# Loading the first weight matrix by three groups in halves, and solving the order table again

## The chip, the cores and the metric

The kernel runs on one core of a Trainium2 chip. The metric is the time of one execution in microseconds (us) on the device; the median of several executions stands for a kernel. The profile comes from one such execution, and its span is some 1.8 us shorter than the time. All runs told of here are runs of one core, in the state that the records call fast.

## The reference, cut to what matters

```python
q_s = exp(q - max(q, -1));  q_s /= sum(q_s, -1)      # softmax over d
k_s = exp(k - max(k, 2));   k_s /= sum(k_s, 2)       # softmax over the sequence
kv  = einsum('bhsd,bhse->bhde', k_s, v)
x   = einsum('bhsd,bhde->bhse', q_s, kv)             # -> [4608 tokens, 512]
h   = x @ w_in                                       # [512, 2048], called W1 below
g   = where(h > 0, h, exp(min(h, 0)) - 1)            # ELU
out = g @ w_out                                      # [2048, 512], called W2 below
```

q, k and v are [8, 8, 576, 64] in fp32. The two products with W1 and W2 are nearly all of the work: 576 matmuls of 128x512 each.

## The kernel before

The tokens go through in 9 blocks of 512. In each block, W1's 2048 columns are 8 groups of 256. A group is 8 matmuls into PSUM, an exp on ACT, and one or two operations on DVE that make GT, the input of the product with W2. Block 0 is special: W1 is still being loaded. Its first two groups are split in two halves over the inner dimension, so that PE can start with the half of x (XT) that is ready first, and with the half of W1 that lands first.

```python
# program(): q, k, v of the first two units on SP's queue, then W1 on POOL's
for g0, g1, half in ((0, 2, 0), (0, 2, 1), (2, 5, None), (5, 8, None)):
    self.load_w1(g0, g1, half, -30, [gate, self.ident] if half == 0 else ())
# ... (load_w1 makes two transfers of each entry: eight in all)
key = 0
turns = [3, 1, 2, 0, 3, 1, 0, 2]                 # PSUM buffers of the groups
for half in range(2):
    for g in range(2):
        self.hg_mm(0, g, turns[g], key, half)    # the two split groups
for g in range(8):
    self.hg(0, g, turns[g], key, "da"[g % 2], g > 1)
    # ...
```

The program only lists operations. In which order each engine runs them is in a table, one list of operation numbers for each engine, that an offline solver made from assumed durations:

```python
ORDER = {
    "pe": ("30 28 32 45 43 47 50 67 54 68 69 70 77 81 85 92 114 102 89 128 136 ..."),
    "dve": ("4 0 5 2 6 7 25 26 27 37 38 39 40 41 42 36 46 49 51 52 53 56 72 73 ..."),
    # ... act, gp, sp
}
```

`fill()` walks through that order with the same assumed durations and, where PE would idle early on, puts in spare 128x128 matmuls of the identity (no result is used) to keep PE's clock up. `spare_after` names what they wait for:

```python
S.spare_after = [self.ident]
# fill(), for each PE operation o until the first large matmuls:
idle = o.start - free - 150
count = int(idle / 80)
if count > 1 and all(d.end < free for d in self.spare_after):
    p = Op("pe", count * 57, self.spare(count), 0)
```

Of the kernel before, what the change touches and what calls it, by code (L numbers as in the profile page):

```python
# [21 lines left out]
ISSUE = {"sp": 550, "act": 550, "gp": 740}  # L22
ORDER = {
    "pe": (
        "30 28 32 45 43 47 50 67 54 68 69 70 77 81 85 92 114 102 89 128 136 127 135 129 137 106 130 "
        "138 108 149 151 125 148 156 133 131 155 150 139 157 152 145 172 174 158 171 173 232 238 237 "
        "236 243 191 242 244 250 249 248 200 255 256 202 262 254 261 211 267 260 266 268 320 312 308 "
        "349 219 332 316 324 390 337 279 328 281 333 411 341 290 345 398 298 350 403 394 416 399 437 "
        "407 424 412 429 361 420 363 425 478 433 372 499 380 438 486 491 482 504 487 512 495 449 525 "
        "500 451 517 508 513 460 571 521 468 563 526 567 576 572 597 584 580 589 537 602 585 593 610 "  # L30
        "539 635 598 548 606 643 555 611 648 639 644 656 652 621 669 623 657 661 665 674 682 687 631 "
        "678 633 670 695 708 691 700 683 704 713 696 734 721 739 717 709 726 730 747 722 760 743 735 "
        "752 765 748 756 773 761 778 769 774 786 782 787 791 792 796 800 804 "),
    "act": (
        "3 22 33 23 24 29 31 34 35 44 48 55 71 74 75 78 82 83 86 93 94 96 103 115 90 91 118 97 116 "
        "107 126 119 132 134 159 162 178 153 146 179 165 229 168 230 175 204 187 233 239 240 190 272 "
        "245 251 252 201 214 257 203 210 263 212 264 283 217 216 321 313 269 213 309 220 354 317 278 "
        "325 292 293 280 391 338 329 289 334 282 295 296 342 291 346 365 351 299 360 395 375 417 442 "
        "404 400 377 374 408 413 362 421 364 378 426 371 479 373 430 434 381 453 439 483 463 492 530 "
        "505 488 448 465 496 466 450 501 459 518 452 509 514 461 462 522 469 564 541 527 568 577 573 "  # L40
        "536 551 615 581 550 603 590 538 586 594 625 540 553 547 636 554 549 599 607 612 556 640 620 "
        "645 649 622 653 624 662 666 658 630 632 675 688 679 671 692 684 701 714 705 697 634 718 740 "
        "710 727 731 723 744 736 753 749 757 766 762 770 779 775 783 788 793 797 801 805 807 "),
    "dve": (
        "4 0 5 2 6 7 25 26 27 37 38 39 40 41 42 36 49 46 51 52 53 56 72 73 76 79 80 84 87 88 95 99 "
        "104 105 100 101 121 117 109 122 110 111 123 140 141 142 154 147 181 182 183 231 176 177 205 "
        "234 235 192 206 193 241 194 207 195 196 246 197 247 253 273 274 275 258 259 265 270 284 271 "
        "285 310 311 286 221 355 222 223 224 225 226 318 319 326 327 330 356 331 335 336 357 343 344 "
        "347 348 352 366 353 300 396 301 302 367 397 401 368 402 303 304 409 410 305 414 415 443 422 "
        "444 423 427 428 445 435 436 454 382 440 455 383 384 441 385 386 484 456 485 387 489 490 497 "  # L50
        "498 531 502 503 510 511 515 516 523 532 524 533 528 529 470 569 570 542 574 471 472 575 473 "
        "543 474 475 544 582 583 587 595 588 616 596 617 618 600 601 608 609 626 613 614 557 558 641 "
        "642 559 560 561 646 562 627 647 654 628 655 659 667 668 660 680 681 672 673 693 694 685 686 "
        "706 707 698 699 719 720 711 712 732 733 724 725 745 737 738 746 750 751 758 759 763 764 771 "
        "772 776 777 784 785 "),
    "gp": (
        "1 14 15 16 17 18 19 20 21 57 59 58 60 63 61 62 66 98 64 65 112 113 124 120 144 143 180 185 "
        "188 "),
    "sp": (
        "8 9 10 11 12 13 184 186 161 164 163 170 167 189 199 198 208 166 169 160 209 215 276 277 315 "  # L60
        "227 218 314 287 228 288 294 358 393 297 359 339 322 323 340 306 307 405 369 376 392 406 370 "
        "379 418 432 419 447 480 481 431 446 388 389 464 507 458 506 493 457 494 520 476 566 477 535 "
        "534 467 565 519 545 546 604 552 578 591 579 619 592 650 637 605 638 629 651 690 676 663 664 "
        "677 703 715 702 689 742 716 755 754 741 728 729 767 768 781 780 789 795 790 794 803 799 802 "
        "798 806 "),
}


# [171 lines left out]
class Gen:  # L240
# [85 lines left out]
    def load_w1(self, g0, g1, half, key, after=()):  # L326
        w = self.w_in.rearrange("(h kc d) f -> h d kc f", h=2, d=D)
        sl = slice(g0 * 256, g1 * 256)
        ks = slice(0, 4) if half is None else slice(2 * half, 2 * half + 2)
        xs = (0, 1) if half is None else (half,)  # L330
        for h in range(2):
            self.S.add("gp", ISSUE["gp"], lambda e, h=h: e.dma_start(  # L332
                self.W1[h:128:2, ks, sl], w[h, :, ks, sl]), key,
                W=[f"W1_{g}{x}{h}" for x in xs for g in range(g0, g1)],
                dma=f"w1{g0}{xs[0]}{h}", nbytes=(len(xs) * (g1 - g0) << 17) * (1.15 if g0 == 2 else 1), after=after,
                follow=self.gpq)
            self.gpq = self.S.ops[-1]

# [281 lines left out]
    def program(self):  # L620
# [7 lines left out]
            if (n, t) == (0, "k"):  # L628
                gate = S.ops[-1]
        loaded = S.ops[-1]  # L630
        for g0, g1, half in ((0, 2, 0), (0, 2, 1), (2, 5, None), (5, 8, None)):
            self.load_w1(g0, g1, half, -30, [gate, self.ident] if half == 0 else ())
            S.ops[-2].behind = loaded
        AB, C, D_ = 3, 2, 1
# [100 lines left out]
        def piece(blocks):  # L735
            if steps:
                for n, go in steps.pop(0):
                    go()
# [6 lines left out]
        key = 0  # L745
        turns = [3, 1, 2, 0, 3, 1, 0, 2]
        for half in range(2):
            for g in range(2):
                self.hg_mm(0, g, turns[g], key, half)
        for g in range(8):  # L750
            self.hg(0, g, turns[g], key, "da"[g % 2], g > 1)
            if g == 4:
                self.side(AB, key, self.ao_mm(0, 1, AB), self.ao_mm(1, 1, AB, 64))
                self.xt(0, 1, AB, key)
                self.xt(1, 1, AB, key, at=64)
            key += 1
            if g >= 5:
                piece(0)
# [79 lines left out]
```

## Time and profile before

| what | where read | value |
|---|---|---|
| time, median of 3 runs | times | 301.82 us |
| PE busy | engine shares | 285.5 of 300.2 us |
| full clock granted | clock record | 12.80 us |
| first matmul with W1 | PE's timeline | 14.78 us |
| wait for W1 | PE's waits | 1.28 us, to 20.96 us |
| group 3 of block 0 starts | PE's timeline | 22.92 us |
| group 6 of block 1 starts | PE's timeline | 66.68 us |
| last large matmul starts | PE's timeline | 296.26 us |

The first matmul with W1 and the last three rows are the ruler of this study. At each of these places the same number of matmuls with W1 has been done in every kernel below, and from group 3 of block 0 to group 6 of block 1 all 14 profiled kernels have the same 88 matmuls with W1, 78 with W2 and 176 small ones to do. So a difference between two of these places is lost or gained in between.

The way in is the PE engine: it is busy 95% of the span, so look only for what it waits for. How the transfers are cut is in the list of DMA issues of the kernel before (operands, queue, count, size of one, median us from issue to landing):

```profile
W<-in_moe_w_in_dram POOLq DMA_DIRECT2D x4, 768.0 KB, 10.3
...
W<-in_moe_w_in_dram POOLq DMA_DIRECT2D x4, 256.0 KB, 4.9
```

The four small ones are the halves of groups 0 and 1; the four large ones are groups 2 to 4 and 5 to 7. The wait of 1.28 us is for the second of the large ones.

### The profile page before, as it was taken

What the parts mean: (1) busy time and instruction counts of PE and PEld (TensorE: products, weight loads), DVE (VectorE), ACT (ScalarE), POOL (GpSimd) and SP (SyncE); (2) the same over time, 40 slices, a digit from 0 to 9 for tenths busy, and PEclk for the clock granted to TensorE, in tenths of its full rate; (3) what the DMA queues carried; (4) which work ended last, traced back from release to release, by engine and by line L of the source; (5) the groups of instructions that cost most, each with busy time, mean ns of one, the idle gap of its engine ahead of it and who ended that gap; (6) DMA issues with size and microseconds to landing.
All of it is one profiled execution on the core that took longest, in us unless ns stands there. A gap on an engine that the chain in (4) does not pass through costs nothing.

```text
span 300.2 us, 4404 instructions
## 1 busy us (share of the span) xinstructions
PE 285.5 (95%) x1846; PEld 234.1 (78%) x1846; DVE 188.8 (63%) x244; ACT 181.5 (60%) x211; POOL 22.1 (7%) x33
## 2 busy tenths in 40 slices
PE   0789999999999999999999999999999999999995
PEld 0658877878888888888888888888888888888883
DVE  2957954898496768766767783878355436565500
ACT  5847948989868676673966677835441623434211
POOL 0950155100000000000000000000000000000000
PEclk9999999999999999999999999999999999999999
DMA  7999996999367593569931958203221201031224
GB/s 263 387 382 391 389 359 234 309 284 265 105 212 240 126 311 70 188 143 239 295 67 41 261 149 227 59 2 70 59 58 29 61 11 35 0 90 38 49 52 105
DMA packets 35283, 49.96 MB, mean 166 GB/s; under 512 B 16320, under 2 KB 16320, under 8 KB 35264
## 3 DMA queue, kind: packets, MB, share of 16 engines
q1 hardware_dynamic: 29680, 34.09, 41.0%
q0 software_dynamic: 5504, 15.47, 15.9%
q8 instruction: 14, 0.23, 0.3%
q10 hardware_dynamic: 80, 0.13, 0.1%
q14 instruction: 5, 0.04, 0.0%
HBM read 36.70 MB, written 9.44 MB: 154 GB/s over the span
## 4 chain that ended last, share of the span: by engine, by line
PE 88%; DMA 5%; DVE 4%; POOL 1%; ACT 1%; SPq 0%; issue 0%
PE PS L588 43%; PE PS L543 40%; DMA W<-in_moe_w_in_dram 3%; PE PS L487 3%; DMA KR<-in_k_dram 2%; PE PS L456 1%; DVE GT L578 1%; POOL W L332 1%; DVE ESB L576 1%; DVE QS L380 0%; DVE ZQ L372 0%; DVE GT L572 0%; DVE MBLK L469 0%; ACT ESB L559 0%; PE PS L403 0%; SPq L315 0%
## 5 line engine op out<-in xcount | busy, mean ns | idle before, releaser
L543 PE MATMUL PS<-XT,W 128*128 128x512 f32 x576 | 140.8, 391 | 1.9 <-DMA W<-in_moe_w_in_dram 1.3
L588 PE MATMUL PS<-W,GT 128*128 128x512 f32 x576 | 141.2, 391 | 0.0
L543 PEld LDWEIGHTS PS<-XT,W 128*128 128x128 f32 x576 | 106.9, 188 | 25.1 <-DMA W<-in_moe_w_in_dram 1.7
L588 PEld LDWEIGHTS PS<-W,GT 128*128 128x128 f32 x576 | 107.1, 188 | 21.9 <-DVE GT L572 0.3
L559 ACT ACTIVATE ESB<-PS 128x1024 f32<-128x1024 f32 x72 | 73.6, 1027 | 68.9 <-PE PS L543 67.1
L576 DVE TENSOR_SCALAR ESB<-ESB 128x1024 f32<-128x1024 f32 x64 | 44.1, 691 | 73.3 <-ACT ESB L559 72.8
L578 DVE TENSOR_TENSOR GT<-ESB,PS 128x1024 fp32r<-128x1024 f32 x64 | 77.8, 1218 | 1.8
L605 ACT ACTIVATE OSB<-PS 128x512 f32<-128x512 f32 x32 | 18.6, 596 | 23.8 <-PE PS L588 23.8
L509 ACT ACTIVATE XT<-PS 128x512 fp32r<-128x512 f32 (+6 forms) x32 | 19.4, 609 | 16.5 <-PE PS L487 14.7
L372 DVE TENSOR_REDUCE ZQ<-QR 128x18 f32<-128x1152 f32 x16 | 21.5, 1346 | 5.0 <-ACT QR L352 4.9
L380 DVE TENSOR_TENSOR QS<-QR,RZQ 128x1152 f16<-128x1152 f32 x16 | 21.7, 1356 | 0.3
L352 ACT ACTIVATE QR<-QR 128x1152 f32<-128x1152 f32 x16 | 18.6, 1161 | 3.1 <-DMA QR<-in_q_dram 3.1
L356 ACT ACTIVATE KR<-KR 128x1152 bf16<-128x1152 f32 x16 | 18.5, 1160 | 0.5 <-DMA KR<-in_k_dram 0.5
L487 PE MATMUL PS<-qsT,MBLK 128*128 128x320 f32 (+5 forms) x64 | 14.2, 307 | 0.1
L431 ACT ACTIVATE qsT<-QT 128x1152 fp32r<-128x1152 f16 x12 | 14.0, 1166 | 0.3 <-DMA QT<-QS 0.3
L365 ACT ACTIVATE VB<-VR 128x1152 bf16<-128x1152 f32 (+1 forms) x12 | 13.5, 1125 | 0.8 <-DMA VR<-in_v_dram 0.8
L487 PEld LDWEIGHTS PS<-qsT,MBLK 128*128 128x128 f32 x64 | 11.4, 190 | 3.1 <-DVE MBLK L469 1.1
L572 DVE SCALAR_TENSOR_TENSOR GT<-PS,ESB 128x1024 fp32r<-128x1024 f32 x8 | 9.8, 1222 | 3.6 <-ACT ESB L570 3.6
L403 PE MATMUL PS<-ID,QS 128*128 128x128 f16 x36 | 3.2, 244 | 9.1 <-DVE QS L380 9.1
L403 PEld LDWEIGHTS PS<-ID,QS 128*128 128x128 f16 x36 | 2.5, 112 | 9.6 <-DVE QS L380 9.1
L469 DVE TENSOR_TENSOR MBLK<-PS,RZK 64x128 fp32r<-64x128 f32 x32 | 9.1, 283 | 0.8
L570 ACT ACTIVATE ESB<-ESB 128x1024 f32<-128x1024 f32 x8 | 8.4, 1056 | 0.2
(28 smaller groups left out, 58.8 us busy)
## 6 DMA issues: line engine op xcount, KB each, us to landing
out_dram<-OSB SPq DMA_DIRECT2D x63, 128.0 KB, 2.4
QR<-in_q_dram SPq DMA_DIRECT2D x12, 576.0 KB, 4.9
KR<-in_k_dram SPq DMA_DIRECT2D x12, 576.0 KB, 5.8
VR<-in_v_dram SPq DMA_DIRECT2D x12, 576.0 KB, 5.6
W<-in_moe_w_out_dram POOLq DMA_DIRECT2D x4, 1024.0 KB, 19.3
W<-in_moe_w_in_dram POOLq DMA_DIRECT2D x4, 768.0 KB, 10.3
QR<-in_q_dram POOLq DMA_DIRECT2D x4, 576.0 KB, 11.1
KR<-in_k_dram POOLq DMA_DIRECT2D x4, 576.0 KB, 6.0
```

What stands on the lines that cost most here:

```text
L352: S.add("act", t_act(1152, False), lambda e: e.activation(flat(q), flat(q), AF.Exp), key - 3, X=[f"qR{i}"], follow=self.table)
L356: S.add("act", t_act(1152, False), lambda e: e.activation(ek[:, :, :, :].rearrange("p h c d -> p (h c d)"), flat(k), AF.Exp), key - 2, X=[ ...
L372: S.add("dve", t_dve(1152), lambda e: e.tensor_reduce(self.ZQ[i][:, :, :].rearrange("p h c -> p (h c)"), q[:, :, :, :].rearrange("p h c d ...
L380: S.add("dve", t_dve(1152), lambda e: e.tensor_tensor(qso, q[:, :, :, :], rz, ALU.mult), key - 3, R=[f"qR{i}", f"RZQ{i}"], W=[f"QS{self.al ...
L487: last = e.matmul(P[:, y:y + n_], M[:, f, :], T[:, c0:c1, f * 64:f * 64 + 64], start=True, stop=True)
L509: S.add("act", t_act((h1 - h0) * n_, True), lambda e, dst=dst, src=src: e.activation(dst, src, AF.Copy), key, W=W, X=X)
L543: last = e.matmul(P[:, t * 512:(t + 1) * 512], self.W1[:, kc, tt * 128:(tt + 1) * 128], self.XT[:, kc, rc:rc + BLK], start=(kc == 0), stop ...
L559: S.add("act", t_act(1024, True), lambda e: e.activation(esb[:, :], P[:, :], AF.Exp), key, W=[f"E{i}"], X=banks)
L576: S.add("dve", t_dve(1024, 2), lambda e: e.tensor_scalar(esb[:, :], esb[:, :], 1.0, -1.0, ALU.min, ALU.add), key, X=[f"E{i}"])
L578: S.add("dve", t_dve(1024), lambda e: e.tensor_tensor(gt, esb[:, :], P[:, :], ALU.max), key, R=[f"E{i}"], W=gw, X=banks)
L588: last = e.matmul(dst, GT[:, jj, ts * 128:(ts + 1) * 128], self.W2[:, jj, :], start=(jj == 0), stop=(jj == 15))
L605: S.add("act", t_act(512, True), lambda e: e.activation(osb[:, :], src, AF.Copy), key, W=[f"O{i}0", f"O{i}1"], X=[f"b{bk}"])
```

## The change

PE has done two groups when it must wait for groups 2 to 4. With three groups in the small transfers it has three groups of work before it needs the next transfer, and that next one is smaller. The order table is solved again, with assumed durations in which the loads of W1 may come later.

```diff
-        for g0, g1, half in ((0, 2, 0), (0, 2, 1), (2, 5, None), (5, 8, None)):
+        for g0, g1, half in ((0, 3, 0), (0, 3, 1), (3, 5, None), (5, 8, None)):
...
-   nbytes=(len(xs) * (g1 - g0) << 17) * (1.15 if g0 == 2 else 1)
+   nbytes=(len(xs) * (g1 - g0) << 17) * (1.25 if g0 == 3 else 1)
...
-            for g in range(2):
+            for g in range(3):
                 self.hg_mm(0, g, turns[g], key, half)
...
-            self.hg(0, g, turns[g], key, "da"[g % 2], g > 1)
+            self.hg(0, g, turns[g], key, "da"[g % 2], g > 2)
...
-    "dve": "4 0 5 2 6 7 25 26 27 37 38 39 40 ...
+    "dve": "2 4 5 0 6 7 25 26 37 27 38 39 40 ...   (all five lists are new)
```

`nbytes` only feeds the assumed durations. On DVE, 26 is the reciprocal of the first q's sums, 27 the first scaled q (QS), 37 the second q's sum (ZQ).

> **What bounds the kernel now.** I read the page first (engine shares and the clock row), then the chain of work that ended last, then the waits of PE, then PE's and DVE's timelines of the first 21 us and of 52 to 69 us, and the landing marks of the W1 transfers.
>
> ```profile
> PE 285.5 (95%) x1846; PEld 234.1 (78%) x1846; DVE 188.8 (63%) x244; ACT 181.5 (60%) x211; POOL 22.1 (7%) x33
> ...
> PE PS L588 43%; PE PS L543 40%; DMA W<-in_moe_w_in_dram 3%; PE PS L487 3%; DMA KR<-in_k_dram 2%; PE PS L456 1%; DVE GT L578 1%; POOL W L332 1%; DVE ESB L576 1%; DVE QS L380 0%; DVE ZQ L372 0%; DVE GT L572 0%; DVE MBLK L469 0%; ACT ESB L559 0%; PE PS L403 0%; SPq L315 0%
> ```
>
> PE is the bound, and the chain has little else in it. That a busy PE has little slack is only shown by spacing: the chain's last PE piece is
>
> ```profile
> 280.33 16.33 PE PS L588 x72
> ```
>
> 72 matmuls in 16.33 us, 0.227 us each. The 1152 large matmuls at that pace are 261 us, and nothing in this change alters their number. So the time can only move by what PE idles. PE's waits:
>
> ```profile
> PE PS L403 <- DVE QS L380: 9.1, 1, 9.1
> ...
> PE PS L543 <- DMA W<-in_moe_w_in_dram: 1.3, 1, 1.3
> PE PS L543 <- DVE XT L512: 0.4, 1, 0.4
> PE PS L543 <- DVE GT L578: 0.2, 1, 0.2
> ```
>
> The reader is to see four waits only: 9.1 us before the first real matmul, 0.4 at 14.8 us, 1.3 for a W1 transfer, 0.2 at 66.7 us. Where they lie:
>
> ```profile
> 14.78 1.16 PE L543 MATMUL PS<-XT,W 128*128 128x512 f32 x4 [0.42 <-DVE XT L512]
> 16.05 0.74 PE L487 MATMUL PS<-qsT,MBLK 128*128 128x512 f32 x2
> 16.63 3.05 PE L543 MATMUL PS<-XT,W 128*128 128x512 f32 x12
> 20.96 11.20 PE L543 MATMUL PS<-XT,W 128*128 128x512 f32 x48 [1.28 <-DMA W<-in_moe_w_in_dram]
> ```
>
> At 19.5 us PE has done the two split groups (16 matmuls) and waits for the load of groups 2-4, of which the second transfer lands at 20.92. From 20.96 to 66.5 us there is no wait over 0.15 us, and none from 66.7 us to the end.
>
> **What the Trainium skill says.** "DMA: Bandwidth & Descriptors", Issuing engines are not separate DMA queues: all transfers run on the same 16 DMA engines and interleave, whoever issues them. The trace agrees: from 1 to 25 us the DMAs move about 390 GB/s, and W1's eight transfers land one behind the other (13.01, 13.67, 14.37, 15.02, 17.70, 20.92, 22.88, 24.83 us), although all are issued by 13.2 us. So other cuts of the same bytes change which bytes come first, not when the last come. "Perfetto Trace Analysis", DMA Optimizations: splitting transfers may let some work start sooner, if the engines are idle; here they are not. "TensorE: Matmul & The Clock Gate", Part 1: PE runs at half clock until it was busy for a window of some 3.4 us, and that window runs freely. The trace agrees: the first transpose is at 9.12 us, the clock is granted at 12.80 us, and the spacing of transposes falls from 107 to 56 ns there.
>
> **The change part by part.** Of the 1.3 us: W1's first two groups become three, loaded by halves. Bytes before group 5 are the same (5 groups), so groups 3-4 land where groups 2-4 landed, near 20.9 us (the last of 16 engines is 1.3 us behind the others there, because one 16 KB instruction fetch of 1.03 us sits on it at 18.4 us; I take it that this stays). But PE now has 24 matmuls to do before it needs them, not 16: 8 x 0.227 = 1.8 us more. In the old order group 2 then took 20.96 to 22.92, so group 3 began at 22.92. If the front did not slip, group 3 could begin at 19.5 + 1.8 = 21.3 us: 1.6 us sooner, and no wait for W1.
>
> The halves are half as big again. First halves: 0.79 MB behind the six q/k/v loads (last landed 12.33 us) at about 0.39 MB/us land near 14.3 us, second halves near 16.3 us. They are needed at 14.8 and 17.6 us or later: hidden. Groups 5-7 land at 24.83 us as before; they were needed at 26.56 us and now near 25.2 us: still hidden, by 0.4 us.
>
> The front slips, because the new order table changes DVE's first work. Before:
>
> ```profile
> 6.02 1.35 DVE L372 TENSOR_REDUCE ZQ<-QR 128x18 f32<-128x1152 f32 x1 [4.41 <-ACT QR L352]
> 7.41 0.27 DVE L376 RECIPROCAL RZQ<-ZQ 128x18 f32<-128x18 f32 x1
> 7.71 1.36 DVE L380 TENSOR_TENSOR QS<-QR,RZQ 128x1152 f16<-128x1152 f32 x1
> 8.98 1.35 DVE L372 TENSOR_REDUCE ZQ<-QR 128x18 f32<-128x1152 f32 x1
> ```
>
> Now the second reduce goes ahead of the first QS: QS ends 1.35 us later, at 10.45, and the first transposes begin near 10.5 us, not 9.1. I walk on with the durations of the old trace. The copies of qsT end near 12.4, ACT's exp of the second k 13.45, the second kv product starts near 14.2 (was 13.88). On DVE the copy of qsT now comes before that of XT: XT is ready at 15.2, so the first group starts at about 15.3 (was 14.78). The m step of the second pair ends near 16.2 (was 16.0), and its product starts near 16.3 (was 16.05). From there PE is dense: slip 0.27 us. Group 3 begins at about 21.6 us: **1.3 us gained**.
>
> One loss may come on top. The spare matmuls that keep PE's clock up are placed by the table's planned times: before, 10 of them stood behind the first transposes; now 12 stand ahead of them and wait for nothing but the identity (ready at 1.5 us), so they run at once and warm nothing. With real work from 10.5 us the full clock comes at 13.9 us at the earliest (10.5 + 3.4), perhaps a window later. Each large matmul at half clock costs 0.2 us more; the four of the first group and the product are exposed, at most 0.9 us. If the grant falls anywhere in 13.9 to 17.3 us alike, my estimate is 0.25 us on average. Before, such a loss was swallowed by the 1.28 us wait; now it is not.
>
> Then the stretch from 46 to 67 us. PE comes sooner; do the others follow? The transfers come in a fixed stream: W2's third part lands at 39.01, needed near 39.5; the fourth moves behind k3, to about 43.1, needed at 44.4. Hidden. But block 1 is reordered. Before, group 1 ended first, then 0, 2 and 3 ran without a break. Now out products stand between groups 2 and 3, and need group 0's GT: group 0 ends near 52.1, exp 1.03, min 0.69, max 1.22 with hops give 55.25, and PE is there at about 54.85: 0.4 us of wait. Group 3 needs group 1's buffer, free after another 1.22 us at 56.5: 0.35 us of wait. DVE was all but full here (13.65 of 15 us busy from 52 to 67 us), so it gives little back:
>
> ```profile
> 65.08 0.30 DVE L469 TENSOR_TENSOR MBLK<-PS,RZK 64x128 fp32r<-64x128 f32 x1
> 65.40 1.22 DVE L578 TENSOR_TENSOR GT<-ESB,PS 128x1024 fp32r<-128x1024 f32 x1
> 66.86 1.23 DVE L572 SCALAR_TENSOR_TENSOR GT<-PS,ESB 128x1024 fp32r<-128x1024 f32 x1 [0.23 <-ACT ESB L570]
> ```
>
> The old waits here (0.1 and 0.33 us) fall away. New waits 0.85, old 0.4: about 0.45 us given back. Behind 67 us PE was dense and stays so; same work, same tail.
>
> Sum: -1.3 (W1 wait) + 0.25 (clock) + 0.45 (block 1) = -0.6 us. 301.82 - 0.6 = **301.2 us**.
>
> **The rivals.** (1) The whole 1.6 us is kept: block 1's order was solved with shifted loads in mind, and the walk's waits of 0.3 to 0.4 us are near its error. Against it are DVE's full 52 to 67 us. It would make 300.3. (2) The wait is turned into others: a cold start and DVE in block 1 eat it all. For it speaks that the old order left PE only 0.33 us idle in block 1; against it that each loss is bounded. It would make 301.8 to 302.2. (3) The fetch falls elsewhere and W1 groups 3-4 land 1.5 us sooner: no gain, PE isn't ready before 21.6. (4) A later reordering opens waits behind 67 us; the old trace had none there, each would add some 0.3 us.
>
> **Range and chances.** The floor is PE: even without any of the waits behind 14.8 us (1.3 + 0.4 + 0.2 = 1.9 us) it is 299.9. So faster by over 2% (295.8) is out of reach. Slower by over 2% needs 6 us of new waits; only a bad order over many blocks could do that. Range 300.3 to 302.0, from rivals 1 and 2.
>
> **What would show it right or wrong.** PE's waits no longer list W1 with 1.3 us (or under 0.3). The first transposes start near 10.5 us, the first large matmul near 15.3, group 3 near 21.6. The clock row's grant is at 13.9 us or later. From 52 to 67 us PE idles 0.6 to 1.2 us, on GT of DVE. Behind 67 us nothing. It is wrong if PE still waits for W1, if the front slips by over 1 us, or if waits stand behind 70 us.

## The result, and the profile after

The changed kernel took **301.64 us** (median of 6 runs, 301.10 to 302.35), the kernel before 301.83 in the same rounds (301.77 to 302.95). The ratio is 0.9989, with a 95% interval of 0.9970 to 1.0008: the same. A ratio here is the mean time of one kernel's fast runs over that of the other's of the same rounds, so it is not quite the ratio of the medians.

The first lines of the page of the changed kernel, engine shares and the chain that ended last:

```profile
PE 286.4 (95%) x1849; PEld 235.0 (78%) x1849; DVE 189.3 (63%) x244; ACT 182.1 (61%) x211; POOL 21.7 (7%) x33
...
PE PS L588 44%; PE PS L543 43%; PE PS L487 3%; DMA W<-in_moe_w_in_dram 2%; DMA KR<-in_k_dram 2%; PE PS L456 2%; POOL W L332 1%; ACT ESB L559 1%; DVE GT L572 0%; ACT ESB L570 0%; PE PS L403 0%; SPq L315 0%; ACT OSB L605 0%
```

By engine, PE's share of the chain went from 88 to 91% and DVE's from 4 to 0. PE's waits in the changed kernel (line waited at, releaser, us in total, times, longest):

```profile
PE PS L403 <- DVE QS L380: 6.6, 1, 6.6
PE PS L653 <- POOL ID L293: 1.9, 1, 1.9
PE PS L543 <- DMA W<-in_moe_w_in_dram: 0.6, 1, 0.6
PE PS L588 <- DVE GT L578: 0.4, 1, 0.4
PE PS L543 <- DVE XT L512: 0.3, 1, 0.3
```

The reader is to see that the wait for W1 has not gone: 1.3 became 0.6. The wait of the first line is shorter than before only because 12 spares now run ahead of it, at 1.9 us, as soon as the identity is there. And a wait of 0.4 for GT is new. Where these lie is in PE's timeline of the changed kernel (start, length, operation; in brackets the idle time before it and what ended that):

```profile
9.94 1.14 PE L403 MATMUL PS<-ID,QS 128*128 128x128 f16 x9 [6.60 <-DVE QS L380]
...
15.09 1.20 PE L543 MATMUL PS<-XT,W 128*128 128x512 f32 x4 [0.29 <-DVE XT L512]
16.12 0.63 PE L487 MATMUL PS<-qsT,MBLK 128*128 128x512 f32 x2
16.59 1.07 PE L543 MATMUL PS<-XT,W 128*128 128x512 f32 x4
18.23 2.09 PE L543 MATMUL PS<-XT,W 128*128 128x512 f32 x8 [0.57 <-DMA W<-in_moe_w_in_dram]
...
55.71 1.19 PE L588 MATMUL PS<-W,GT 128*128 128x512 f32 x4 [0.39 <-DVE GT L578]
56.99 1.21 PE L543 MATMUL PS<-XT,W 128*128 128x512 f32 x4
```

The wait is no longer for groups behind the split ones. It is at 18.2 us, inside the split groups, for their **second half**. The landing marks say why. A transfer is spread over 16 DMA engines. Fifteen of them had the second half in by 16.4 us; the last landed at 17.99. One engine had been a microsecond behind most of the others since 7.5 us: two packets, at 5.6 and 6.2 us, took 529 and 622 ns, and two more took 538 and 688 ns in this transfer. (The trace gives no engine's number with a packet; that these packets are all that one engine's is inferred from their times.)

The Trainium skill, "DMA: Bandwidth & Descriptors", Why a DMA increments its semaphore by 16 and not by 1, says that the engines finish independently and that only the full count means that all data has landed. The trace agrees, and puts a size to it: the slowest engine of one transfer came more than 1.5 us behind the other fifteen.

Against the ruler:

| place | before | changed | difference |
|---|---|---|---|
| full clock granted | 12.80 | 13.67 | |
| first matmul with W1 | 14.78 | 15.09 | +0.31 |
| group 3 of block 0 | 22.92 | 21.99 | -0.93 |
| group 6 of block 1 | 66.68 | 66.21 | -0.47 |
| last large matmul | 296.26 | 295.92 | -0.34 |

Of 0.93 us gained at group 3, half is given back by group 6 of block 1. That stretch, in one row for each kernel: length; busy time of PE, PEld, DVE, ACT and POOL; granted clock; DMA share; GB/s. The kernel before:

```profile
22.92:66.68 43.76, 43.59 (x344) 34.51 (x342) 32.20 (x44) 35.03 (x40) 10.66 (x12) 1.00 1.08 331
```

and the changed kernel:

```profile
21.99:66.21 44.22, 43.75 (x343) 34.65 (x341) 34.01 (x45) 35.12 (x41) 9.55 (x11) 1.00 1.09 341
```

The same PE work takes 0.46 us longer at the same clock. DVE has 1.8 us more work in this stretch, but that is not why PE waits for it at 55.7 us: from 52 to 67 us DVE was as busy as before (13.67 and 13.65 of 15 us), and it took up group 0's two operations at once, 0.03 us after ACT's exp of that group had ended at 53.68 us. From the last matmul of group 0 to its GT, ACT and DVE run without a pause. ACT and then DVE in the changed kernel:

```profile
52.65 1.94 ACT L559 ACTIVATE ESB<-PS 128x1024 f32<-128x1024 f32 x2 [0.16 <-PE PS L543]
...
53.71 0.69 DVE L576 TENSOR_SCALAR ESB<-ESB 128x1024 f32<-128x1024 f32 x1
54.44 1.22 DVE L578 TENSOR_TENSOR GT<-ESB,PS 128x1024 fp32r<-128x1024 f32 x1
```

### The profile page after: what moved, and what is told of

It is laid out like the page before. It is cut to its first block, busy times and chain, and to the rows that moved or that the text cites. A ratio compares the mean times of both kernels' runs of the same rounds, so it can differ in the third digit from the quotient of the medians.

```text
span 300.0 us, 4412 instructions
## 1 busy us (share of the span) xinstructions
PE 286.4 (95%) x1849; PEld 235.0 (78%) x1849; DVE 189.3 (63%) x244; ACT 182.1 (61%) x211; POOL 21.7 (7%) x33
## 4 chain that ended last, share of the span: by engine, by line
PE 91%; DMA 5%; ACT 1%; POOL 1%; DVE 0%; SPq 0%; issue 0%
PE PS L588 44%; PE PS L543 43%; PE PS L487 3%; DMA W<-in_moe_w_in_dram 2%; DMA KR<-in_k_dram 2%; PE PS L456 2%; POOL W L332 1%; ACT ESB L559 1%; DVE GT L572 0%; ACT ESB L570 0%; PE PS L403 0%; SPq L315 0%; ACT OSB L605 0%
## 5 line engine op out<-in xcount | busy, mean ns | idle before, releaser
L509 ACT ACTIVATE XT<-PS 128x512 fp32r<-128x512 f32 (+6 forms) x32 | 19.5, 608 | 7.8 <-PE PS L487 7.3
```

The costliest lines, as they stand in the source:

```text
L509: S.add("act", t_act((h1 - h0) * n_, True), lambda e, dst=dst, src=src: e.activation(dst, src, AF.Copy), key, W=W, X=X)
```

## The experiments

Two theories stood. **A**: the re-solved table loses what the cut gains, because block 1 has waits built into its order. **B**: the front loses it, by the swap on DVE, the useless spares and a late clock, and what is behind is chance. All kernels below gave the right result. The times of all of them come first, with the median of the kernel before from the same call. By the record's rule of 2% all twelve are "the same" as the kernel before; what is told apart below is read from the intervals and the ruler. In the call of e5 to e8 the kernel before had three slow runs (304.06 to 304.56 us), so the four ratios of that call flatter the kernels tried; the medians are the better guide there.

| kernel | median us | before | ratio, 95% interval |
|---|---|---|---|
| e1: new cut, old table | 301.40 | 302.01 | 0.9974 [0.9954, 0.9995] |
| e2: old cut, new table | 303.01 | 302.01 | 1.0044 [1.0007, 1.0081] |
| e3: changed, swap on DVE undone | 301.34 | 302.01 | 0.9975 [0.9958, 0.9993] |
| e4: changed, spares late | 301.43 | 302.01 | 0.9973 [0.9955, 0.9992] |
| e5: changed, two SP entries moved | 301.68 | 302.08 | 0.9975 [0.9938, 1.0012] |
| e6: e5, swap undone, early spares | 303.26 | 302.08 | 1.0011 [0.9971, 1.0051] |
| e7: e1 and early spares | 301.12 | 302.08 | 0.9949 [0.9914, 0.9984] |
| e8: before and early spares | 301.65 | 302.08 | 0.9969 [0.9930, 1.0008] |
| e9: changed, again | 301.72 | 301.91 | 0.9988 [0.9957, 1.0018] |
| e10: old table, finer cut | 301.52 | 301.91 | 0.9981 [0.9951, 1.0011] |
| e11: e10 and early spares | **300.81** | 301.91 | 0.9960 [0.9928, 0.9991] |
| e12: changed, swap undone, early spares, two holds moved | 301.94 | 301.91 | 1.0004 [0.9973, 1.0035] |

Every profiled run on the ruler, as us at the first matmul with W1, then us from place to place:

| kernel | table | first | to group 3 | to group 6, block 1 | to the last | last at |
|---|---|---|---|---|---|---|
| before | old | 14.78 | 8.15 | 43.75 | 229.58 | 296.26 |
| e1 | old | 15.92 | 6.39 | 43.73 | 229.60 | 295.65 |
| e7 | old | 14.89 | 6.76 | 43.74 | 229.76 | 295.15 |
| e8 | old | 14.54 | 7.52 | 43.72 | 229.78 | 295.56 |
| e10 | old | 15.55 | 6.55 | 43.72 | 230.65 | 296.47 |
| e11 | old | 14.46 | 6.54 | 43.79 | 229.74 | 294.54 |
| changed | new | 15.09 | 6.89 | 44.23 | 229.71 | 295.92 |
| e9 | new | 15.43 | 6.26 | 44.23 | 230.05 | 295.97 |
| e2 | new | 15.18 | 9.75 | 45.34 | 230.37 | 300.63 |
| e3 | new | 15.16 | 6.20 | 44.77 | 229.87 | 296.00 |
| e4 | new | 14.88 | 6.23 | 44.22 | 230.69 | 296.02 |
| e5 | new | 15.41 | 6.28 | 44.20 | 231.00 | 296.88 |
| e6 | new | 14.85 | 7.07 | 44.19 | 231.11 | 297.22 |
| e12 | new | 14.75 | 6.62 | 44.21 | 230.24 | 295.82 |

### e1: the new cut with the old table

```diff
# the changed program; ORDER of the kernel before, its operation numbers shifted:
# 69, 70 -> +1;  71..76 -> +2;  77 -> "69 72" (the group now split);  78 and up -> +1
```

> The new cut of W1 and the three split groups, with the order table of the kernel before (its entries renumbered, group 2's eight matmuls in two halves where they stood). Theory A (the cut removes the 1.3 us wait, the new order table gives 0.8 us of it back: front slip, waits in block 1): first large matmul at 14.8 us as before, group 3 at 21.3 to 21.6, no W1 wait over 0.3 us, PE waits from 46 to 67 us under 0.6 us in all, time 300.4 to 300.9. Rival B (whatever PE gains before 46 us is lost in block 1, because DVE, POOL and the transfers there do not come sooner, whatever the order): PE waits from 46 to 67 us of 1.3 us or more, time 301.5 to 301.9.

Measured: 301.40 us, ratio 0.9974. PE's timeline of e1 at the front:

```profile
15.92 1.15 PE L543 MATMUL PS<-XT,W 128*128 128x512 f32 x4 [0.57 <-DVE XT L512]
17.05 0.72 PE L487 MATMUL PS<-qsT,MBLK 128*128 128x512 f32 x2
17.61 8.72 PE L543 MATMUL PS<-XT,W 128*128 128x512 f32 x37
```

There is no wait for W1 at all; the second half landed at 16.57. In this execution the front was the slowest of all (15.92 us, with the full clock only at 14.76), and still the end came earlier than in the changed kernel, because from group 3 on it lost nothing against the kernel before: 43.73 and 229.60 us against 43.75 and 229.58. This speaks for A. The median is 0.5 us above the range that I had named for A, and just under B's.

### e2: the old cut with the new table

```diff
# the kernel before; ORDER of the changed kernel, renumbered the other way round
```

> The old cut of W1 and two split groups, with the new order table (renumbered). Theory A: the W1 wait of 1 to 1.3 us at 20.9 us stays, the new waits of block 1 (0.4 and 0.1 us at 55 to 57 us) stay too, time 302.0 to 302.5. Rival B: the order table of itself is neutral and the waits of block 1 shrink as PE comes later: 301.7 to 301.9.

Measured: 303.01 us, ratio 1.0044, slower than the kernel before, and more than either theory had it. The profiled execution was its slowest, 306.47 us; the other five took 302.40 to 303.38. PE's waits in it have one line that is worse than anything above:

```profile
PE PS L543 <- DMA W<-in_moe_w_in_dram: 2.7, 1, 2.7
```

and the stretches around that wait, with the granted clock as the last number but two:

```profile
14.00:22.00 8.00, 5.37 (x61) 3.83 (x59) 4.52 (x8) 4.79 (x6) 6.52 (x9) 1.00 1.11 345
22.00:24.00 2.00, 1.53 (x6) 1.29 (x7) 1.43 (x2) 0.00 (x0) 0.00 (x0) 0.95 1.24 397
24.00:27.00 3.00, 3.00 (x8) 2.34 (x7) 0.74 (x2) 1.02 (x1) 0.00 (x0) 0.50 1.29 392
27.00:30.00 3.00, 3.00 (x14) 2.44 (x13) 1.17 (x1) 1.93 (x2) 0.00 (x0) 0.96 1.34 391
```

PE got through 8 matmuls from 24 to 27 us, where 13 would fit at full clock: the wait of 2.74 us cost the clock as well, from 23.82 to 27.23 us, and each matmul took 427 ns there and not 227. The Trainium skill, "TensorE: Matmul & The Clock Gate", Part 1, What's actually happening, says that the clock is decided in windows of 3.413 us that run freely. This run agrees to the hundredth: the clock was granted at 13.58 us, and 13.58 + 3 x 3.413 = 23.82. Of the window that ended there (20.41 to 23.82) PE was idle until 22.47, 60% of it.

So a wait for W1 that fills as much of a window as here is dearer than its length. In the profiled run of before it was 1.28 us, 38% of a window, and the clock stayed. What made the wait so long here is that the second transfer landed at 22.43 us, and not at 20.92; whether the new table or chance did that is not shown, and only the 0.38 us of waiting for GT at 59.8 us are surely the table's. In 4 of the 39 timed runs of the kernel before in this study the time was 304.04 to 304.56 us and the mean clock 0.993 to 0.994, as in e2's slow run (0.993); the other 35 took at most 303.11 us, and their clock, where it was recorded, was 0.997 or more. In 0.6% of 302 us, 1.8 us are lost, which is a half clock for 3.6 us: one window. None of the 12 runs of the changed kernel (two calls), nor of the 54 of the other kernels with the new or the finer cut, had a clock under 0.997. Those slow runs of the kernel before were not profiled: that they had e2's long wait is argued, not shown. If it is so, the change takes away a tail of some 2.5 us that the median doesn't see.

### e3 and e4: is it the front?

e3 puts the first QS back ahead of the second sum; the spares then fall behind the first transposes again, as before. e4 lets the changed kernel's spares wait for the first q's reciprocal, and has 24 of them there and not 12.

```diff
# e3, DVE's list
-  "2 4 5 0 6 7 25 26 37 27 38 ...
+  "2 4 5 0 6 7 25 26 27 37 38 ...
# e4
-        S.spare_after = [self.ident]
+        S.spare_after = [self.ident, S.ops[26]]
```

> The changed kernel with one swap undone: DVE divides the first q (QS) before it sums the second. The spare matmuls then stand behind the first transposes again. Theory A: first transposes at 8.6 to 9.1 us, first large matmul 0.2 to 0.3 us sooner than in the changed kernel (14.8), time 0.2 to 0.4 us less: 301.2 to 301.4. Rival C (the front is set by the last k and v loads and DVE's later steps, or by the W1 halves, so the swap costs nothing): within 0.1 us of the changed kernel, 301.5 to 301.8.

> The changed kernel with 24 spare matmuls, not 12, that wait for the first 1/ZQ (7.4 us), so PE is busy from 7.4 us to the first transposes. Theory D (the spread of 301.1 to 302.35 us of the changed kernel is the time at which PE gets its full clock): clock granted near 11 us, spread under 0.4 us, median 301.2 to 301.5. Rival E (the spread comes from transfers, a DMA engine that falls behind by 1 us or not): the clock comes sooner but the spread stays near 1 us, median 301.5 to 301.7.

Measured: 301.34 and 301.43 us, ratios 0.9975 and 0.9973. The first matmul with W1 came at 15.16 us in e3, where the swap is undone, and at 15.09 in the changed kernel: **the swap on DVE costs nothing there**. Why, is in DVE's timeline of the changed kernel:

```profile
7.15 0.27 DVE L376 RECIPROCAL RZQ<-ZQ 128x18 f32<-128x18 f32 x1
7.33 1.29 DVE L372 TENSOR_REDUCE ZQ<-QR 128x18 f32<-128x1152 f32 x1
8.54 1.35 DVE L380 TENSOR_TENSOR QS<-QR,RZQ 128x1152 f16<-128x1152 f32 x1
9.80 0.26 DVE L376 RECIPROCAL RZQ<-ZQ 128x18 f32<-128x18 f32 x1
10.10 1.36 DVE L380 TENSOR_TENSOR QS<-QR,RZQ 128x1152 f16<-128x1152 f32 x1
```

The first matmul with W1 needs both units, so it waits for what the second QS leads to. Ahead of the end of the second QS stand the same six operations of DVE in either order: it ended at 11.46 us here and at 12.02 in the kernel before, 0.26 us of it because q had been loaded sooner. Only the first QS is later, and nothing hung on it alone.

e4's spares brought the full clock at 11.27 us, yet its six times still spread over 0.98 us. So the spread of the changed kernel is not the time of that grant alone, as rival E had it.

Both runs reached group 3 early (21.36 and 21.12 us, no wait for W1), and both gave most of it back: their last matmul, at 296.00 and 296.02, is not before the changed kernel's. So B explains where a few tenths go in the front, but not the end. The two also show two more places of the new order. In e3, ACT:

```profile
61.69 1.17 ACT L431 ACTIVATE qsT<-QT 128x1152 fp32r<-128x1152 f16 x1 [1.06 <-DMA QT<-QS]
62.77 1.01 ACT L559 ACTIVATE ESB<-PS 128x1024 f32<-128x1024 f32 x1
```

ACT stood idle for a DMA transpose, with the exp of group 4 behind it in the list, ready at 62.12 us. In e4, DVE and then PE:

```profile
73.68 1.22 DVE L572 SCALAR_TENSOR_TENSOR GT<-PS,ESB 128x1024 fp32r<-128x1024 f32 x1 [3.21 <-DMA out_dram<-OSBX]
...
74.96 1.19 PE L588 MATMUL PS<-W,GT 128*128 128x512 f32 x4 [0.87 <-DVE GT L572]
```

GT of group 7 is written over the buffer from which block 0's output is stored, and the store is late in SP's list: DVE waits 3.2 us, PE 0.87.

### e5 and e6: move the entries that hold

e5 puts the transpose of unit 4 ahead of the four entries before it in SP's list and the store that held group 7 further up. e6 is e5 with the swap undone and with 28 spares that wait for the exp of the first q, so that they run at once ahead of the first transposes.

```diff
# e5, SP's list
-  "8 9 10 11 12 13 170 187 161 164 171 185 165 190 200 168 162 199 209 210 216 167 219 ...
+  "8 9 10 11 12 13 170 185 187 161 164 171 165 190 200 168 162 167 199 209 210 216 219 ...
# e6, fill(): ahead of the first PE operation
+            if o.eng == "pe" and first:
+                p, first = Op("pe", 0, self.spare(first), 0), 0        # 28
+                p.deps = {d: "raw" for d in self.warm_after}           # identity, exp of the first q
```

> The changed kernel with two entries of SP's order moved: the DMA transpose of q pair 4 goes ahead of the load and of the three block 0 stores that stood before it, and the store of row part 2 of block 0, which stood behind the second transpose, goes right behind the other stores. Theory F (with the new table, what PE gains in the front is given back in block 1 to transfers that SP issues late: the transpose holds ACT and so group 4's exp, the store holds group 7's GT): the transpose lands near 58 us, not 61, the store under 66 us, not 72.7; alone, at the changed kernel's front, 0 to 0.3 us: 301.3 to 301.6. Rival G (DVE's full load alone gives it back): no change at all, and group 6 of block 1 still waits for GT at 66 us.

> The same SP order, DVE's first swap undone, and 28 more spare matmuls behind the first exp of q (5.9 us), so PE is busy from 5.9 us. The front is then as soon as can be: group 3 at 21.0 to 21.3 us. Theory F: the gain of the front is kept to the end, last large matmul at 295.0 to 295.3, time 300.6 to 301.0. Rival G: it is lost again in block 1 as in the runs with the front mended alone (e3_qs_first, e4_spares_late): last large matmul at 295.9 to 296.1, time 301.3 to 301.5.

Measured: 301.68 us for e5, 303.26 for e6: **a miss**. The waits of the entries that I moved went, and others came. In e5's PE timeline:

```profile
72.00 0.61 PE L487 MATMUL PS<-qsT,MBLK 128*128 128x384 f32 x2 [0.39 <-ACT qsT L431]
```

Now the transpose of the next unit is late: it landed at 70.77 us, and in e9, the changed kernel again with the same front, at 68.84, though its issue began at 63.59 us in both. That the store moved ahead of it does this is likely, not shown. In e6 the same wait was 0.76 us, and the second half of W1 was late as well (0.79 us). Three of e6's runs also spent 0.2 to 0.7 us more than usual outside the span; by the spans alone it is still 1.0 us slower than the kernel before (medians 301.3 and 300.3). Behind group 6 of block 1 both took 231 us, the longest of all.

### e7 and e8: early spares with the old table

```diff
# e7 = e1, e8 = the kernel before, both with e6's 28 early spares
```

> The new cut with the old order table (e1_cut_oldorder) and the 28 early spare matmuls. There the clock came only at 14.8 us and the first large matmul at 15.9. Theory D (the clock's grant moves the front): clock granted by 12.5 us, first large matmul at 14.8, group 3 at 21.3, and as the old table lost nothing after group 3, last large matmul near 294.7, time 300.2 to 300.7. Rival E: grant is sooner but the time stays 301.2 to 301.5.

> The kernel before with the 28 early spare matmuls alone. Theory A (the W1 wait at 20 us swallows whatever the front gains): the W1 wait is there, 1.0 to 2.5 us, and the time is within 0.3 us of the kernel before. Rival D (the front's clock is what costs): 0.5 us or more faster.

Measured: 301.12 us for e7, ratio 0.9949 (by the medians 0.96 us less than the kernel before), and 301.65 for e8, ratio 0.9969 (0.43 us less, between what its two theories had). The wait for W1 was 0.83 us in e8. The full clock came at 11.73 and 9.26 us. e7's waits (its line numbers are 5 higher):

```profile
PE PS L548 <- DMA W<-in_moe_w_in_dram: 0.4, 1, 0.4
...
PE PS L548 <- DVE GT L583: 0.2, 1, 0.2
```

The wait for the second half is back, 0.43 us, and not only because PE is there sooner: the half landed at 17.65 us, and in e1 at 16.57. The record shows what the early spares did to it. In each profiled run one fetch of instructions (a packet of 16 KB in a queue of its own, 0.95 to 1.16 us long) falls among the loads of W1. In the five runs with early spares it comes at 14.1 to 15.5 us, in the other nine at 17.4 to 19.5: 28 spares more bring PE's list forward. In e6, e7 and e12 it falls into the second half, and its last engines land 1.0 to 1.4 us behind most or all of the others; PE was there at 17.3 to 17.5 us and would not have waited for a half that lands by 16.7 us, as it did in e1, e3, e4, e5 and e9. That the late engine is the one with the fetch is inferred from the times.

Behind group 3 only the old table's 0.17 us is left. The gain here seems the old table's, since e6 and e12, with the same spares and the new table, gained nothing; but those two changed SP's list as well, and no run has the early spares alone on the new table.

### e9 to e12: the change again, and a cut with one more piece

e9 is the changed kernel once more. e10 keeps the old table and two split groups and gives group 2 a transfer of its own; e11 adds the early spares. e12 takes all I had found in the new table at once: the swap undone, early spares, the conversion that held ACT moved behind the exp, and the store that held DVE moved up behind an entry that is due earlier.

```diff
# e10, the kernel before with
-        for g0, g1, half in ((0, 2, 0), (0, 2, 1), (2, 5, None), (5, 8, None)):
+        for g0, g1, half in ((0, 2, 0), (0, 2, 1), (2, 3, None), (3, 5, None), (5, 8, None)):
# e11 = e10 with 28 early spares
# e12, the changed kernel with e6's front and
-  act  "... 180 240 241 191 246 215 ..."      sp  "... 199 209 210 216 167 219 ..."
+  act  "... 180 240 241 246 191 215 ..."      sp  "... 199 209 167 210 216 219 ..."
```

> The changed kernel itself once more, as the measure of the three others of this call. Expected: 301.3 to 301.8 us median; of the kernel before some runs above 303 us (a W1 wait long enough to lose the full clock), of this one none.

> The kernel before (two split groups, old order table) with the load of groups 2-4 cut in two, group 2 and groups 3-4: W1 in ten transfers, not eight. Theory A (what counts is that group 2 is there in time; a third split group isn't needed): group 2's load lands at 16.5 to 18 us, no W1 wait over 0.3 us at group 2, group 3 at 21.3 to 21.6, nothing lost after it with the old table, last large matmul near 294.8, time 300.3 to 300.9. Rival H (more transfers, or the one slow DMA engine, move the wait to groups 3-4, which land at 20.5 to 21.5): a W1 wait of 0.3 to 1 us at group 3, time 301.0 to 301.6.

> The same with the 28 early spare matmuls (the clock granted by 12.5 us, not up to 15). Theory D: as e10_fine_cut or up to 0.4 us better, spread under 0.6 us; 300.2 to 300.7. Rival: no better than e10_fine_cut, as DVE and ACT set the first group's start.

> The changed kernel with the fast front (DVE's swap undone, 28 early spares), ACT's widening of q pair 4, which waits for the DMA transpose, moved behind group 4's exp, and the late block 0 store moved ahead of two loads on SP. Theory F (the new table's loss behind group 3 beyond its two waits at 55 to 57 us is ACT held by the transpose and GT held by that store): from group 3 to the last large matmul 273.9 us or less, as in the changed kernel, last one at 295.0 to 295.4. Rival I (the table has more such places, every one of them close): 274.3 us or more again.

Measured: e9 301.72 us, ratio 0.9988, so the first result stands. In its profile PE had no wait for W1 (the second half landed at 16.67) and group 3 was 0.3 us sooner than in the first profile; the end was not. PE's timeline of e9:

```profile
55.41 1.19 PE L588 MATMUL PS<-W,GT 128*128 128x512 f32 x4 [0.39 <-DVE GT L578]
...
74.88 1.21 PE L588 MATMUL PS<-W,GT 128*128 128x512 f32 x4 [0.32 <-DVE GT L572]
```

The first line is the main finding. In all eight profiled kernels with the new table (changed, e2, e3, e4, e5, e6, e9, e12) PE's idle time at this place is 384 or 385 ns, whether group 3 of block 0 began at 21.12 or 24.93 us; none with the old table has it. A wait that keeps its length when everything ahead of it moves is made by the order itself: PE does the matmuls of group 0, asks for its GT too soon, and the way over ACT and DVE has a fixed length. The second line is e4's wait for the store, smaller.

e12 took 301.94 us, ratio 1.0004: nothing gained. Its spans have a median of 300.0 us, against 300.1 for the kernel before; two of its runs spent 0.7 and 1.2 us more outside the span than usual. In its profile the holds are gone, but its front waited 0.83 us for XT and 0.33 for the second half, and the 0.385 us stayed. That wait I had not taken away: it needs the table solved otherwise. From group 3 to the last large matmul it took 274.45 us, no less than the changed kernel's 273.94: rival I's mark, and not theory F's.

e10 took 301.52 us, ratio 0.9981, less than e1. Its profiled run shows that the old table can lose too: a q load and then a v load came late, ACT stood still for them until 74.17 and 75.72 us, and PE waited in turn. ACT and then PE in e10:

```profile
74.17 1.17 ACT L352 ACTIVATE QR<-QR 128x1152 f32<-128x1152 f32 x1 [1.10 <-DMA QR<-in_q_dram]
75.72 1.17 ACT L365 ACTIVATE VB<-VR 128x1152 bf16<-128x1152 f32 x1 [0.38 <-DMA VR<-in_v_dram]
...
80.93 0.47 PE L487 MATMUL PS<-qsT,MBLK 128*128 128x192 f32 x2 [0.34 <-ACT KR L356]
```

e11 took **300.81 us** (300.47 to 301.21), ratio 0.9960, less than both kernels: 1.1 us under the median of the kernel before, and its slowest run is below that median. Its interval overlaps those of e7, e8 and e10, so that it is the best of them is not shown. PE's timeline of e11's front:

```profile
6.13 3.02 PE L659 MATMUL PS<-ID 128*128 128x128 f16 x28 [6.13 <-ACT QR L357]
...
14.46 1.17 PE L548 MATMUL PS<-XT,W 128*128 128x512 f32 x4 [0.29 <-ACT XT L514]
15.74 0.72 PE L492 MATMUL PS<-qsT,MBLK 128*128 128x512 f32 x2
16.30 8.95 PE L548 MATMUL PS<-XT,W 128*128 128x512 f32 x38
```

The spares bring the full clock at 8.87 us, the first matmul with W1 comes sooner than in any other run, and W1 is never waited for: group 2 and its neighbours land one small piece at a time (16.89, 17.56, 18.93, 20.26 us).

## Why the prediction was right, and where its sizes were off

The predicted 301.2 us was 0.44 us too low; the range and "the same" held. The terms of the sum were the right ones, but one was half as large, one acted elsewhere, and one of the named signs of being wrong came true: PE still waited for W1. That the total stayed within half a microsecond is in part luck, since the errors of the terms went both ways, and the range was wide beside the effect. The terms can be checked one by one on the profiled runs.

- **The front slips by 0.27 us.** The first matmul with W1 was foreseen at 15.3 us and came at 15.09, 15.43 in e9. Of the two reasons given, the swap on DVE is neutral (e3). The other holds: DVE now copies qsT (13.75 to 14.44 us) ahead of its half of XT, which was foreseen ready at 15.2 us and was ready at 15.04, 0.37 us after ACT's half. The first transposes, foreseen at 10.5 us, began at 9.94: 0.26 us of that is q, loaded sooner in this run, the rest shorter gaps between DVE's operations. What else moves the front is the clock, in the point after next: over all profiled runs without early spares the first matmul with W1 lies between 14.78 and 15.92 us.
- **The W1 wait, -1.3 us.** Groups 3 and 4 never were waited for, as foreseen. But the halves were called hidden, and the second half was not: 0.57 us in the changed kernel. So this term was -0.7 and not -1.3 us. **This is the term that was mis-sized.** It put the landing near 16.3 us from a mean rate, and fifteen of sixteen engines kept to that; the wait is set by the sixteenth. (That mean rate, about 390 GB/s, is the trace's from 3 us on; from 1 us, as the prediction has it, the mean is 364.) In six of the profiled runs with the new cut and an unchanged or undone front (changed, e1, e3, e4, e5, e9) it came once, in all three with early spares (e6, e7, e12) again, with 0.79, 0.43 and 0.33 us: there by the fetch of instructions told of under e7.
- **The clock, +0.25 us.** It was granted at 13.67 us (13.9 or later was foreseen), ahead of the first large matmul. The same goes for every other profiled run: the grant came between 8.87 and 15.19 us, and always ahead of the first matmul with W1. So it cost nothing where the prediction put the cost, in the large matmuls. But PE's small work before them is on the way to the first large one, and it is slower without the full clock. The second unit's transposes and the product that follows them, in the kernel before:

```profile
12.73 0.71 PE L403 MATMUL PS<-ID,QS 128*128 128x128 f16 x9
13.25 0.70 PE L487 MATMUL PS<-qsT,MBLK 128*128 128x512 f32 x2
```

and in the changed kernel:

```profile
12.11 1.17 PE L403 MATMUL PS<-ID,QS 128*128 128x128 f16 x9
13.04 1.00 PE L487 MATMUL PS<-qsT,MBLK 128*128 128x512 f32 x2
```

Over the 14 profiled runs the first matmul with W1 follows the grant: 14.46 to 14.89 us in the seven granted by 12.80, 15.09 to 15.18 in the three at 13.28 to 13.67, 15.41 to 15.92 in the four at 14.51 or later. The early spares alone (e1 to e7, before to e8, e10 to e11) brought it forward by 1.03, 0.24 and 1.09 us. How much of the changed kernel's own slip of 0.31 us is the clock's, and how much is the copy on DVE, is not separated.
- **Block 1, +0.45 us.** Foreseen as waits of 0.4 near 55 us on group 0's GT and 0.35 at 56.5 us. Measured: 0.385 us at 55.71 and 0.09 at 56.99 us, with the dents that each leaves in the spacing 0.55 and 0.25 us; net of what the old table lost, +0.47. PE's idle time from 52 to 67 us was 0.47 us; 0.6 to 1.2 had been foreseen. The runs confirm the step better than any other: six runs with the old table take 43.72 to 43.79 us for this stretch, six of the eight with the new one 44.19 to 44.23; the other two are e2, at half clock for part of it, and e3, with ACT held.
- **Behind 67 us nothing.** It was +0.13 us in the changed kernel and +0.47 in e9, where the store of block 0 is late. The wait behind 70 us, named as what would make the prediction wrong, was there in e9, small (0.32 us at 74.88).

The profile adds up: +0.31 - 1.26 + 0.48 + 0.13 = -0.34 us at the last matmul. The prediction had -1.05 for the first two terms together and -0.6 for all. The span shows -0.2 us and the medians -0.19, because the end behind the last matmul took 0.1 us more in the profiled run.

So theory A holds for about half of what the cut gains, by a wait that is built in; the new table's other losses, 0.1 to 1.5 us behind 66 us, go, where the traces name a wait, with a transfer that lands late. What is not settled: why single packets of one DMA engine take so long in some executions; how much of the 0.4 us (by the ratios) between e3 or e4 and the changed kernel is real, since their intervals overlap and e12 contradicts it; and what the four slow runs of the kernel before looked like inside.

## What to carry to other kernels

Change the cut of a load and the order of the work in separate runs: here the cut alone gained 0.6 us by the medians, the order alone, on the old cut, lost 1.0, and together they looked like nothing. A wait that keeps its length while everything ahead of it moves belongs to the order, and a wait that comes and goes belongs to a transfer; the first is mended in the table, the second by smaller first pieces (e10 and e11 never waited for W1). Look where the fetches of instructions fall: 28 spares moved one forward by 1.9 to 4.2 us (e1 to e7, e10 to e11, before to e8), and in e7 into a transfer that PE then waited for. When work waits for a whole transfer, reckon with its slowest engine, and mind a wait for a load that fills much of a clock window: at 60% of one it cost the clock as well, at 38% it didn't.

## What the Trainium skill lacked or had wrong

- "TensorE: Matmul & The Clock Gate", Part 1, says that the clock falls back after an idle window of some 3.4 us. In e2 a wait of 2.74 us was enough: the window that cost the clock had PE idle for 2.06 us and busy for 1.35 us, and half the clock then lasted 3.41 us. In the kernel before, 1.28 us idle in a window did not cost it. The page gives no such share.
- The same part gives the time to the full clock as about one busy window. From the first transposes on (or from the early spares on) it took from 2.7 us (e11) to 5.9 us (e7) here. That fits windows that run freely: counted back from the grant, in e9 a window with PE at work for its last 1.5 us did not grant it, nor in e7 one with 2.5 us, and in e11 one with 2.7 us did.
- "DMA: Bandwidth & Descriptors" says that the 16 engines finish independently, but not by how much. Here the last engine came over 1.5 us behind the other fifteen in one transfer of 384 KB, after single packets of 529 to 688 ns; PE waited 0.57 us for it.
- "Runtime: NRT & Kernel Launch", Instruction fetch mechanics, calls the cost of crossing into the next 16 KiB of instructions mostly hidden. In the kernel before PE was at work all through the fetch (16.63 to 19.68 us); but a fetch took 0.95 to 1.16 us of a DMA queue among the loads of W1 in each of the 14 profiled runs. In the kernel before it came at 18.36 us, and the transfer that PE waited for landed at 20.92 us, 1.29 us after fifteen of its sixteen engines. In e1, with no other late engine, the last one fell from 0.04 to 1.05 us behind the fifteenth over a fetch of 1.12 us. With 28 early spares the fetch came sooner (17.40 to 15.51 us from e1 to e7), and PE waited 0.33 to 0.79 us for the second half in e6, e7 and e12.
